# An H3 convolution with a feed-forward block on one core: short convolution on array halves, kept weight groups, and a new hand-off order

## The chip, the cores and the metric

The kernel runs on one core of one Trainium2 chip. The metric is the device time in microseconds of one execution. Before the change three runs gave 260.77, 261.48 and 261.54 us, median 261.48. Where a part of the program is meant, the engines are named as in the profile: PE is TensorE (PEld its weight loads), DVE is VectorE, ACT is ScalarE, POOL is GpSimd, SP is SyncE, which here only starts transfers.

## What is computed

All arrays are bfloat16: q, k, v of 2048 x 640, a short filter of 4 taps per channel, a long filter of 2048 taps per channel, and the feed-forward weights for F = 1728.

```
x = A_q;  q = layernorm(x)
k_shift = sum over t = 0..3 of k_pad[t : t + S] * shift_k[:, 3 - t]       # short causal convolution
kv = k_shift * v
y  = causal convolution of kv with ssm_k (length 2048)  +  kv * ssm_D
h  = x + q * y
h2 = h + (silu(layernorm(h) @ w_gate) * (layernorm(h) @ w_up)) @ w_down
```

## The kernel before

The sequence is cut into four blocks of 512. A block is held as 128 partitions of 4 rows (R = 4) of D = 640 = 5 x 128 columns. The feed-forward width is cut into seven groups of 256 columns (the last has 192), so 13 full chunks of 128 and a tail of 64.

The long convolution is done block by block by a discrete Fourier transform written as matmuls. For block j: the filter's block is loaded and transposed (g, gT), its spectrum G_j is made by matmuls with the constant WF (`spectrum`, line L375 in before, L353 after); the window H_j = G_j plus or minus G_(j-1) is formed on VectorE; kv_j comes from the short convolution and a multiply by v; its spectrum X_j is made in the same way; then the sums over i of X_i * H_(j-i) are accumulated in a spectrum A (`mac`: products L746, accumulations L747 in before; L619 and L622 after; L719 / L598 make the first products). The inverse transform (`inverse`: first sums on VectorE L823/L826, matmuls with WI L878; after L697/L700 and L748) gives y, which is multiplied into the normalised rows (L892 / L762) and added to x (h, L905 / L765). A layer norm follows, h is transposed (hT), and the feed-forward f_j runs: gate and up matmuls (L1022 / L852), ScalarE and VectorE turn them into the hidden tile tT (L1012, L1014, L1016), and the down projection (L1110 / L906) adds it up. f_j is written so that it lies beside the convolution work of block j+1.

A spectrum needs sums and differences of partial transforms. One of G_0's transforms is taken "directly" in before: a second constant matrix of 512 KB (`const_minus`, in tile tT) gives it by 16 more matmuls. The others get it from partial sums on VectorE.

The short convolution is done by TensorE with diagonal matrices of the taps. In block 0 each of the 4 row blocks takes 5 x 4 matmuls of 128 partitions and 128 columns (L639). In blocks 1 to 3 each row block takes 20 matmuls of 64 columns (L648): a tile T holds k twice, once shifted by a row, so that 128 partitions carry 64 channels at two taps. T's second half is made by a copy on ScalarE (L565) and transfers T<-T; the table `pairs` for it is filled on GpSimd (L1185) from taps turned by four small matmuls (L1175). Three "spins" of matmuls on constants (L1151, 18, 16 and 16) stand ahead of the real work.

What sets the order: every operation is recorded in a plan with a nominal duration in nanoseconds (for instance 1120 for one row block of L639, 640 for one of L648, named TWONS). The list ORDER gives the sequence in which they are handed to the engines; a negative number means that the operation takes its second engine. Each engine and each queue works in order, so ORDER fixes what stands behind what. Buffers are slots (12 'big' of 640 KB, 8 'S', 4 pairs of PSUM banks 'ps', 5 'row', 2 'co'), and a load must wait until its slot is free. In `add_into` a sum is made by a transfer that adds to its destination, issued by GpSimd (L278; after L255); a transfer of 640 KB is given 3830 ns in the new plan. Weight loads (L959 / L810) are issued by SP, or by GpSimd for blocks named in GLOAD.

Of the kernel before, what the change touches and what calls it, by code (L numbers as in the profile page):

```python
# [31 lines left out]
ADDLO = ('G1', 'G2', 'X1', 'X2', 'X3')  # L32
ADDMAC = ()
ADDWIN = (1,)
ADDH = (1, 2)
LEAD = {}
PAD = 16
DIRECT = ('G0',)
ACTLN = 0
ACTKV = 0  # L40
ACTLN2 = (0, 1, 2, 3)
LN1DVE = ()
LN2POOL = (1, 2)
HTURN = (1, 3, 2)
GTURN = (3,)
KTURN = (1, 2, 3)
SUM = {'X3': 'four', 'i2': 'four', 'i3': 'four', 'G3': 'four'}
ADDP = {(1, 1): ((0, 1),)}
ADDINV = (2,)
WHOLE3 = False  # L50
WARMUP = (18, 16, 16)
MERGE = ()
WIDE = ()
H1ACT = ()
PAIRED = True
K0TURN = False
EARLY = True
FFN4 = True
KVPAIR = ()
DPOOL = False  # L60
LASTCUT = 2
DIAGDVE = 4
ATURN = ()
GLOAD = (1, 2, 3, 'T')
FIRST = False
TWOTAPS = True
TWONS = 640
TCOPY = (1, 2)
# [43 lines left out]
HALVES = (ROWS[:2], ROWS[2:])  # L112


def make_basis():

# [96 lines left out]
def kernel(ctx: ExitStack, tc: tile.TileContext, A_q, A_k, A_v, A_shift_k, A_ssm_k, A_ssm_D, B_x,  # L213
# [369 lines left out]
    def load_k(j):  # L583
        if TWOTAPS and j:
            return load_two(j)
# [745 lines left out]
```

## Time and profile before

| what | value |
|---|---|
| median of 3 runs (lowest, highest) | 261.48 us (260.77, 261.54) |
| profiled execution: span from first to last instruction | 259.6 us |
| the rest of a run's median beside that span | 1.9 us |
| PE / DVE / ACT / POOL busy | 251.3 / 198.6 / 180.0 / 97.0 us |
| first feed-forward matmul | 49.70 us |
| last matmul ends, then last sum and store | 256.1 us, 3.5 us |
| bytes moved | 45.38 MB |
| granted TensorE clock | 1.000 |

The profile gives the span of the one execution that was profiled; its own time outside the span isn't listed, so times are compared through the 1.9 us. In the tables of groups a row has line, engine, operation, output and inputs, shape and count, then busy time and mean duration in ns, then the idle time just before and who ended it. In a timeline a row has start, length, engine, line, names, count. Matmuls overlap in the pipe, so the length of one is longer than the distance from its start to the next one's. The rows of waits give engine and line, whom it waited for, the total, how often, and the longest.

### The profile page before, as it was taken

The page shows a single profiled execution, that of the slowest core. Times are in us where ns is not written, and L with a number is a line of the kernel's source. Part 1 is how long each engine was busy: PE and PEld are TensorE (multiplying, and loading weights), DVE is VectorE, ACT ScalarE, POOL GpSimd, SP SyncE. Part 2 cuts the span into 40 slices and gives each one's busy share as a digit, 9 for nine tenths or more (in the row PEclk, how much of TensorE's full clock was granted, in tenths as well). Part 3 has the DMA queues.
Part 4 walks back from the last instruction along what each step waited for, and adds up shares of the span by engine and source line. Part 5 has one row for each costly group of instructions (what it writes and reads, how often), then busy time and mean ns, then how long its engine had stood idle before and what let it go on. Part 6 is the DMA issues. An engine that isn't in the chain of part 4 may idle for free.

```text
span 259.6 us, 4700 instructions
## 1 busy us (share of the span) xinstructions
PE 251.3 (97%) x1803; PEld 154.2 (59%) x1818; DVE 198.6 (77%) x259; ACT 180.0 (69%) x297; POOL 97.0 (37%) x115
## 2 busy tenths in 40 slices
PE   8999899999998999999999999999999999999994
PEld 7967577654654477754465477544456764444663
DVE  4679999999998999999999999999998200004403
ACT  2899999999998998569855985655497134637200
POOL 7961300008914199926117962240951022000000
PEclk9999999999999999999999999999999999999999
DMA  6997999979999998999997965994498546000002
GB/s 218 403 251 119 289 252 340 280 115 279 247 238 168 182 217 204 190 191 201 214 231 110 299 151 107 198 238 130 100 215 255 101 77 70 8 0 0 13 15 76
DMA packets 64752, 45.38 MB, mean 175 GB/s; under 512 B 31014, under 2 KB 60267, under 8 KB 64731
## 3 DMA queue, kind: packets, MB, share of 16 engines
q1 hardware_dynamic: 58896, 32.96, 51.1%
q0 software_dynamic: 5824, 12.13, 24.9%
q8 instruction: 14, 0.23, 0.4%
q14 instruction: 8, 0.06, 0.1%
q10 hardware_dynamic: 10, 0.01, 0.0%
HBM read 30.01 MB, written 4.59 MB: 133 GB/s over the span
## 4 chain that ended last, share of the span: by engine, by line
PE 78%; ACT 9%; DMA 6%; DVE 2%; issue 2%; SPq 1%; ACTq 0%; DVEq 0%
PE ps L1022 40%; PE ps L1110 23%; PE ps L375 10%; DMA big<-in_B_w_up_dram 4%; PE ps L878 3%; DMA big<-in_A_q_dram 3%; ACT T L565 2%; ACT big L364 1%; ACT S L364 1%; PE ps L648 1%; ACT row L757 1%; ACT big L664 1%; ACT big L473 1%; ACT tT L1014 1%; DVE row L892 1%
## 5 line engine op out<-in xcount | busy, mean ns | idle before, releaser
L1022 PE MATMUL ps<-big,big 128*128 128x512 bf16 x525 | 119.9, 379 | 1.7 <-DMA big<-in_B_w_up_dram 0.8
L1022 PEld LDWEIGHTS <-big 128*128 128x128 bf16 x540 | 52.5, 98 | 61.1 <-DMA big<-in_B_w_up_dram 1.3
L1110 PE MATMUL ps<-wd,tT 128*128 128x320 bf16 (+1 forms) x416 | 60.3, 299 | 0.0
L1110 PEld LDWEIGHTS <-tT 128*128 128x128 bf16 x416 | 40.7, 98 | 16.3
L1016 DVE TENSOR_TENSOR tT<-tT,co 128x2048 bf16<-128x2048 bf16 x12 | 14.5, 1219 | 34.4 <-ACT tT L1014 32.4
L375 PE MATMUL ps<-big,WF 128*128 128x320 bf16 x240 | 39.1, 299 | 1.3 <-ACT big L364 1.0
L1012 ACT CAST co<-ps 128x1024 bf16<-128x1024 f32 x24 | 24.2, 1011 | 17.3 <-PE ps L1022 16.8
L747 DVE TENSOR_TENSOR S<-S,big 128x2560 bf16<-128x2560 bf16 x23 | 34.3, 1492 | 1.2 <-DMA S<-big 0.5
L746 DVE TENSOR_TENSOR big<-S,S 128x2560 bf16<-128x2560 bf16 x23 | 34.1, 1485 | 0.2
L375 PEld LDWEIGHTS <-WF 128*128 128x128 bf16 x240 | 23.1, 97 | 12.8 <-issue 2.3
L1014 ACT ACTIVATE tT<-ps 128x1024 bf16<-128x1024 f32 x24 | 24.5, 1029 | 8.8 <-PE ps L1022 8.7
L757 ACT ACTIVATE row<-big 128x640 bf16<-128x640 bf16 x32 | 23.5, 742 | 1.8 <-DMA big<-in_A_q_dram 1.1
L807 ACT ACTIVATE row<-big,sm 128x640 bf16<-128x640 bf16 x23 | 20.3, 922 | 3.8 <-POOL sm L789 2.8
L1117 POOL DMA_DIRECT2D out_dram<-row x12 | 11.8, 1010 | 29.2 <-ACT row L1116 29.1
L364 ACT CAST S<-ps 128x320 bf16<-128x320 f32 (+1 forms) x36 | 19.4, 583 | 0.3
L1116 ACT CAST row<-ps 128x640 bf16<-128x640 f32 x12 | 8.1, 691 | 14.2 <-PE ps L1110 13.2
L364 ACT ACTIVATE big<-ps 128x640 bf16<-128x640 f32 (+1 forms) x24 | 15.6, 696 | 0.7 <-PE ps L375 0.7
L278 POOL DMA_DIRECT2D big<-row x8 | 7.0, 919 | 22.9 <-DVE row L892 22.9
L892 DVE SCALAR_TENSOR_TENSOR row<-row,ps 128x640 bf16<-128x640 bf16 x16 | 12.8, 815 | 1.1 <-PE ps L878 0.9
L278 POOL DMA_DIRECT2D S<-big x2 | 2.5, 1266 | 26.3 <-DVE S L719 19.1
L719 DVE TENSOR_TENSOR big<-S,S 128x2560 bf16<-128x2560 bf16 (+1 forms) x10 | 12.2, 1218 | 0.1
L959 POOL DMA_DIRECT2D big<-in_B_w_gate_dram x8 | 9.1, 1137 | 8.1 <-PE ps L1022 7.8
(110 smaller groups left out, 330.4 us busy)
## 6 DMA issues: line engine op xcount, KB each, us to landing
big<-in_B_w_up_dram SPq DMA_DIRECT2D x17, 320.0 KB, 5.1
big<-in_B_w_gate_dram SPq DMA_DIRECT2D x16, 320.0 KB, 4.7
big<-in_A_ssm_k_dram SPq DMA_DIRECT2D x4, 640.0 KB, 9.2
big<-in_A_q_dram SPq DMA_DIRECT2D x4, 640.0 KB, 7.6
big<-in_A_v_dram SPq DMA_DIRECT2D x4, 640.0 KB, 6.9
big<-in_B_w_gate_dram POOLq DMA_DIRECT2D x8, 320.0 KB, 7.2
big<-in_B_w_up_dram POOLq DMA_DIRECT2D x7, 320.0 KB, 6.7
wd<-in_B_w_down_dram SPq DMA_DIRECT2D x1, 2080.0 KB, 12.2
```

The source lines that it names most:

```text
L364: (lambda: nc.scalar.activation(dst(), src(), ACT.Copy, scale=2.0)) if twice else (lambda: nc.scalar.copy(dst(), src())),
L375: nc.tensor.matmul(ap(ps)[:, h, 0:NH], w, ap(src)[:, r, h * NH:(h + 1) * NH], start=(first and i == 0), stop=(last and i == len(rs) - 1), ...
L746: nc.vector.tensor_mul(flat2(b), X.part(xs), H.part(hs))
L747: f(A.part(dst), A.part(dst), flat2(b))
L757: act(825, lambda r=r, junk=junk: nc.scalar.activation(ap(junk), ap(x)[:, r, :], ACT.Square, scale=D ** -0.5, accum_out=sm(s, 1)[:, r:r + ...
L807: nc.scalar.activation(ap(row), ap(x)[:, r, :], ACT.Identity, bias=sm(s, 5)[:, r:r + 1], scale=sm(s, 4)[:, r:r + 1])
L892: nc.vector.scalar_tensor_tensor(two(ap(t)), two(ap(t)), 1.0, half(ap(ps)), op0=ALU.mult, op1=ALU.mult, accum_out=sm(s, 0)[:, r:r + 1])
L1012: act(1010, lambda ps=ps: nc.scalar.copy(ap(co)[:, at:at + 2, :], ap(ps)), src, [(co, gi % 2)])
L1014: act(1010, lambda ps=ps: nc.scalar.activation(ap(tT)[:, c:c + 2, :], ap(ps), ACT.Silu), src, [done(range(c, c + 2), ROWS)])
L1016: dve(1220, lambda: nc.vector.tensor_mul(ap(tT)[:, c - 2:c + 2, :], ap(tT)[:, c - 2:c + 2, :], ap(co)), [co], [done(range(c - 2, c + 2), R ...
L1022: nc.tensor.matmul(ap(ps)[:, i, :], ap(w)[:, k, off:off + P], ap(hT)[:, k, :], start=(k == 0), stop=(k == KT - 1))
L1110: nc.tensor.matmul(ap(ps)[:, hf, to:to + n], t, ap(wd)[:, c, col + (hf - hs[0]) * NH:col + (hf - hs[0]) * NH + n], start=(c == order[0]), ...
```

## The change

1. `DIRECT` is empty. G_0 gets its last part by two subtractions on VectorE as the other spectra do; the matrix `const_minus` and its load and the 16 matmuls with it go.
2. The short convolution has one form in all blocks. T holds k once. A row block takes 40 matmuls, each of 64 partitions by 64 columns, partitions 0 to 63 and 64 to 127 in turn, into two PSUM banks (L577). The plan gives it CONVNS = 680. Five diagonal pieces [128, 4, 64] replace both tables; ScalarE's doubling copy, the transfers T<-T, the `pairs` table and the four small matmuls go; a halo of 3 columns is copied instead. In block 0 the fill of the diagonals is 4 pieces on VectorE and 16 on GpSimd.
3. `KEEP = (3, 3, 3)`: the last three weight groups of a block stay in their slots, and odd blocks take the groups in reverse, so that these come first. 9 of 28 group loads go. GLOAD is (0, 1, 2, 3).
4. The third spin goes.
5. `sum_into` replaces `add_into`: any full sum may go to VectorE or to an adding transfer, and the product and the accumulation of `mac` are separate operations. Adding transfers of 640 KB: 4 before, 12 after (10 of them from a 'big' slot into a spectrum); of 160 KB (into h): 8 before, 4 after. VectorE's accumulations L747 / L622: 23 before, 14 after. Of the layer norms' small chains two more go from GpSimd to VectorE; 8 normalising steps move from ScalarE to VectorE; GpSimd issues 22 weight loads instead of 15.
6. ORDER is new: it was searched for the nominal durations alone.

```diff
-DIRECT = ('G0',)
+DIRECT = ()
-WARMUP = (18, 16, 16)
+WARMUP = (18, 16)
-GLOAD = (1, 2, 3, 'T')
-TWONS = 640
+GLOAD = (0, 1, 2, 3)
+KEEP = (3, 3, 3)
+CONVNS = 680
 ORDER = [
-    0, 2, 31, 1, 4, 5, 7, 10, 6, 8, 16, 13, 12, 11, 22, 29, 26, 37, 27, 14, 3, 15, 23, 28, 42, -39, 9, 35, -37, 24, 39, 205, 40,
...
+    0, 4, 2, 8, 1, 5, 21, 6, 52, 46, 50, 7, 48, 3, -48, 22, -52, 54, 14, 20, -54, -10, -14, 30, 18, 49, 28, 24, -30, -26,
...
-    def add_into(to, what, r, w, n=R * D):
-
-        plan.moved("add", P * n * 2, 1280, lambda: nc.gpsimd.dma_start(
-            out=to(), in_=what(), accum_op=ALU.add, max_dma_last_dim=2 * D * 2), r, w)
+    def sum_into(ns, fn, to, what, r, w, n=R * D, dma=False):
+
+        def by_dma():
+            nc.gpsimd.dma_start(out=to(), in_=what(), accum_op=ALU.add, max_dma_last_dim=2 * D * 2)
+        a, b = ("dve", ns, fn), ("add", 958.0 if n == D else 3830.0, by_dma)
+        if dma:
+            a, b = b, a
+        return plan.add(*a, r, w, (), b)
...
             def mm(r=r, out=out):
                 for c in range(KT):
                     for t in range(4):
+                        for b in range(2):
+                            at = slice(b * H2, (b + 1) * H2)
+                            if j:
+                                k = tk()[at, c, PAD + r - t:PAD + r - t + 4 * P - 3:4]
+                            else:
+                                q, off = (r - t, 1) if r >= t else (r - t + 4, 0)
+                                k = tk0()[at, c, q, off:off + P]
+                            nc.tensor.matmul(out()[:, b, c, :], k, ap(diag)[at, c, t, :], start=(t == 0), stop=(t == 3))
+            op = pe(CONVNS, mm, [of_t("H", *QUARTERS) if j else of_t(*FIRSTS), diag], [ps], [kv], 258)
...
-            def go(b=b, xs=xs, hs=hs, dst=dst, f=f):
-                nc.vector.tensor_mul(flat2(b), X.part(xs), H.part(hs))
+            dve(1490, lambda b=b, xs=xs, hs=hs: nc.vector.tensor_mul(flat2(b), X.part(xs), H.part(hs)), [X.at(xs), H.at(hs)], [b], [A.b])
+
+            def go(b=b, dst=dst, f=f):
                 f(A.part(dst), A.part(dst), flat2(b))
-            dve(3010, go, [X.at(xs), H.at(hs)], [b, A.at(dst)])
+            if f == nc.vector.tensor_add:
+                sum_into(1490, go, lambda dst=dst: A.part(dst), lambda b=b: flat2(b), [b], [A.at(dst)])
+            else:
+                dve(1490, go, [b], [A.at(dst)])
...
+        order = GROUPS if j % 2 == 0 else GROUPS[::-1]
+        for n, gi in enumerate(order):
...
+            if j == NB - 1 or n < NGRP - KEEP[j]:
+                kept.pop(gi)
```

Where the order moves, in three queues. First VectorE in the accumulation of block 2, before: each product (L746) is followed by its accumulation (L747) into the spectrum S_66.

```order
L746 TENSOR_TENSOR big_79<-S_68,S_70 128x2560
L747 TENSOR_TENSOR S_66<-S_66,big_79 128x2x1280
L746 TENSOR_TENSOR big_75<-S_71,S_65 128x2560
L747 TENSOR_TENSOR S_66<-S_66,big_75 128x2x1280
L746 TENSOR_TENSOR big_76<-S_71,S_65 128x2560
L747 TENSOR_TENSOR S_66<-S_66,big_76 128x2x1280
L746 TENSOR_TENSOR big_79<-S_71,S_65 128x2560
L747 TENSOR_TENSOR S_66<-S_66,big_79 128x2x1280
```

The same place after. S_66 is again the sum; big_76 and big_74 hold products that a transfer adds.

```order
L619 TENSOR_TENSOR big_76<-S_71,S_64 128x2560
L622 TENSOR_TENSOR S_66<-S_66,big_81 128x2x1280
L501 TENSOR_TENSOR S_68<-big_80,S_68 128x1280
L345 CAST big_83<-ps_92 128x640
L619 TENSOR_TENSOR big_81<-S_69,S_70 128x2560
L622 TENSOR_TENSOR S_66<-S_66,big_81 128x2x1280
L619 TENSOR_TENSOR big_74<-S_71,S_64 128x2560
L619 TENSOR_TENSOR big_82<-S_71,S_64 128x2560
L619 TENSOR_TENSOR big_81<-S_71,S_64 128x2560
L501 TENSOR_TENSOR S_68<-big_80,S_68 128x1280
L504 TENSOR_TENSOR S_68<-S_68,big_83 128x1280
L622 TENSOR_TENSOR S_66<-S_66,big_81 128x2x1280
```

Products without an accumulation behind them (big_76, big_74) are left to transfers; the last row waits until big_76 has been added.

GpSimd's queue in the same stretch, before, from the first transfers of block 2 to its one adding transfer (S_66 <- S_66).

```order
L563 DMA T<-T 64x5x512
L1117 DMA out_dram<-row_88 128x640
L959 DMA big_73<-in_B_w_gate_dram 128x5x256
L563 DMA T<-T 64x5x514
L1117 DMA out_dram<-row_87 128x640
L278 DMA S_66<-S_66 128x2x1280
L959 DMA big_82<-in_B_w_gate_dram 128x5x256
L959 DMA big_80<-in_B_w_up_dram 128x5x256
```

After: four adding transfers into S_66 (L255), with a memset ahead of them and two weight loads (L810) between.

```order
L255 DMA big_82<-row_85 128x640
L970 MEMSET tail 64x512
L255 DMA S_66<-big_72 128x2x1280
L255 DMA S_66<-big_73 128x2x1280
L810 DMA big_73<-in_B_w_up_dram 128x5x256
L810 DMA big_73<-in_B_w_gate_dram 128x5x256
L255 DMA S_66<-big_76 128x2x1280
L255 DMA S_66<-big_74 128x2x1280
```

The weight loads go into slot big_73, so they wait until the transfer that adds big_73 has landed, and the next two adds stand behind them.

SP's first entries, before:

```order
L597 DMA T<-in_A_k_dram 128x2560
L330 DMA big_73<-in_A_ssm_k_dram 128x5x512
L342 DMA big_74<-in_A_q_dram 128x2560
L337 DMA big_75<-in_A_v_dram 128x2560
L1199 DMA WF<-const_wf 128x2048
L342 DMA big_76<-in_A_q_dram 128x2560
L1205 DMA tT_84<-const_minus 128x2048
```

and after:

```order
L308 DMA big_72<-in_A_ssm_k_dram 128x5x512
L514 DMA big_74<-in_A_k_dram 128x2560
L977 DMA WF<-const_wf 128x2048
L320 DMA big_75<-in_A_q_dram 128x2560
L315 DMA big_76<-in_A_v_dram 128x2560
L810 DMA big_78<-in_B_w_up_dram 128x5x64
L308 DMA big_80<-in_A_ssm_k_dram 128x5x512
```

The long filter comes first, then k and WF, and TensorE turns g ahead of k and runs 18 of G_0's matmuls before the short convolution of block 0. The first feed-forward matmul now stands behind all of X_1, G_1, G_2 and the short convolution of block 2: 160 L353 matmuls stand ahead of it (156 L375 before) and 480 matmuls of L577 (80 of L639 and 80 of L648 before).

More of the change, by code (lines that the diff above doesn't have):

```diff
@@ L578, in plain, with load_k, both @@
[L578 to L598 removed]
+    def load_k(j):
+        if j == 0:
+            k = new("ld")
+            load(MB, 5120, lambda: nc.sync.dma_start(out=rd(k), in_=block(kk, j)), [k])
+            return k
+        tiny = plan.add("pool", 600, lambda: nc.gpsimd.tensor_copy(*both()), [halo if j == 1 else of_t(("A", R - 1))], [of_t("H")], (),
+                        ("act", 240, lambda: nc.scalar.copy(*both())))
+        def both():
+            return tk()[:, :, PAD - 3:PAD], ap(halo) if j == 1 else tk()[:, :, TW - 3:TW]
+        turns = []
+        for a in range(R):
+            turns.append(transfer(MB / 4, lambda a=a: nc.sync.dma_start(
+                out=tk()[:, :, PAD + a * P:PAD + (a + 1) * P], in_=kk[j * BLK + a * P:j * BLK + (a + 1) * P, :], transpose=True),
+                [], [of_t(("A", a))]))
+        if j == 1:
+            for op in [tiny] + turns:
+                op.deps.update(firsts)
+        return T
@@ L600, in turned_k @@
     def turned_k(k, behind=None, table=None):
-        if plan.block in KTURN or not plan.block and K0TURN:
+        if plan.block:
             return k
-        src = rd if plan.block else plain
-        kT = T if TWOTAPS else new("kT")
         for r in range(R):
@@ L630, in kv_of, with by_half, out, mm @@
+        return T
+    firsts = []
+    def kv_of(j, v, behind=None):
+        if j == 0:
+            dve(60, lambda: nc.vector.memset(tk0()[:, :, :, 0:1], 0.0), [], [of_t("K0")])
         kv = new("t4")
-        for r in (0, 2, 1, 3) if plan.block in KVPAIR else range(R):
+        def by_half(t):
+            return t.rearrange("p (c b x) -> p b c x", c=KT, b=2)
+        for r in range(R):
             ps = conv_ps()
-            def mm(r=r, ps=ps):
+            def out(ps=ps):
+                return half(ap(ps)).rearrange("p b (c x) -> p b c x", c=KT)
+            def mm(r=r, out=out):
@@ L707, in mac, with straight @@
-    def mac(A, X, H, first, pieces=((0, 1),), adds=(), at=None):
-        if at in MERGE:
-            merged(A, X, H, first, [a for a in adds if isinstance(a, int)])
-            return
-        adds = [a for a in adds if not isinstance(a, int)]
+            if j == 0:
+                firsts.append(op)
+            def straight(r=r, out=out):
+                nc.vector.tensor_mul(by_half(ap(kv)[:, r, :]), out(), by_half(rd(v)[:, r, :]))
+            op = plan.add("act", 700, lambda r=r, out=out: nc.scalar.copy(by_half(ap(kv)[:, r, :]), out()), [ps, v], [(kv, r)], (), ("dve", 820, straight))
@@ L807, in scalar @@
             nc.scalar.activation(ap(row), ap(x)[:, r, :], ACT.Identity, bias=sm(s, 5)[:, r:r + 1], scale=sm(s, 4)[:, r:r + 1])
-        if bias and plan.block >= ACTLN or not bias and plan.block in ACTLN2:
-            plan.add("act", 930, scalar, [(x, r), s], [row], holds, ("dve", 450, vector))
-        else:
-            dve(450, vector, [(x, r), s], [row], holds)
+        plan.add("act", 930, scalar, [(x, r), s], [row], holds, ("dve", 450, vector))
     def inverse(A, x, n1, pieces=((0, 1),), minus=None, groups=(ROWS,)):
@@ L932, in load_w @@
     def load_w(gi):
[L933 to L944 removed]
+        if gi in kept:
+            return kept[gi]
         w = new("wgu")
@@ L1080, in ffn @@
-        first, then = ROWS[:2], ROWS[2:]
-        for gi in range(0, lead, 2):
-            chunks((gi, gi + 1), first)
-        for gi in range(lead, NGRP - 1):
-            by_four(gi) if FFN4 else chunks((gi,), ROWS)
-        behind = odd_by_four() if FFN4 else odd_chunks()
-        for gi in range(0, lead, 2):
-            behind = chunks((gi, gi + 1), then)
+        order = GROUPS if j % 2 == 0 else GROUPS[::-1]
+        for n, gi in enumerate(order):
+            if gi == NGRP - 1:
+                last = odd_by_four()
+            else:
+                close = gi // 2 in [g // 2 for g in order[:n]]
+                if not close:
+                    co = new("co")
+                last = by_four(gi, co, close)
+            if j == NB - 1 or n < NGRP - KEEP[j]:
+                kept.pop(gi)
@@ L1088, in ffn @@
+        behind = last
         for r in ROWS:
             ps = new("ps_f")
-            order = list(range(lead * 2, NCH)) + list(range(lead * 2))
+            order = list(range(NCH))
             last = end and r == ROWS[-1]
@@ L1190 @@
     plan.add("pool", 600, lambda: nc.gpsimd.memset(ap(wd)[64:P, NC_FULL, :], 0.0), [ident], [(wd, "zero")])
-    turns = [op for op in plan.ops if op.eng in ("turn", "aturn")]
     first("Lx0")
     x = load_x(0)
-    if FIRST:
-        plan.ops[-1].then.update(turns)
     first("Lv0")
@@ L1212 @@
     first("k0")
-    k = turned_k(k, spun, table)
-    again = spun
-    if not K0TURN:
-        again = spin(WARMUP[2])
-        again.deps.update(op for op in plan.ops if op.name == "k0" and op.eng == "pe" and op is not again)
-    kv = kv_of(0, k, None, v, again)
+    turned_k(k, spun, table)
+    kv = kv_of(0, v)
     first("g0")
@@ L1248 @@
         stage("Lk")
[L1249 removed]
+        load_k(j)
         stage("Lv")
@@ L1287 @@
         stage("i")
-        s = inverse(A, x, n1, groups=HALVES if LEAD.get(j) else (ROWS,))
+        s = inverse(A, x, n1)
         stage("t")
```

404 lines of the change are left out of this document (77 added, 327 removed), and 72 rows, old and new, of the table ORDER.

## The prediction

> **What bounds the kernel now.** I read the head of the page, then TensorE's share by stage, then its waits. The columns of the windows are the length and, for each engine, the busy time.
>
> ```profile
> span 259.6 us, 4700 instructions
> PE 251.3 (97%) x1803; PEld 154.2 (59%) x1818; DVE 198.6 (77%) x259; ACT 180.0 (69%) x297; POOL 97.0 (37%) x115
> ```
>
> ```profile
> 0.00:49.70 49.70, 46.63 (x507) 36.39 (x508) 41.84 (x94) 42.92 (x93) 19.42 (x44) 1.00 1.00 265
> 49.70:256.10 206.40, 204.67 (x1298) 117.80 (x1311) 156.38 (x166) 137.05 (x205) 77.54 (x71) 1.00 0.72 155
> 256.10:259.60 3.50, 0.00 (x0) 0.00 (x0) 0.41 (x1) 0.00 (x0) 0.00 (x0) 1.00 0.20 67
> ...
> 49.70:100.00 50.30, 49.20 (x340) 28.18 (x343) 48.89 (x46) 48.18 (x77) 24.59 (x20) 1.00 1.02 221
> 100.00:150.00 50.00, 49.74 (x346) 29.04 (x350) 49.25 (x50) 36.91 (x51) 29.10 (x29) 1.00 0.96 199
> ```
>
> ```profile
> PE ps L375 <- ACT big L364: 1.0, 2, 0.8
> ...
> PE ps L1022 <- DMA big<-in_B_w_up_dram: 0.8, 1, 0.8
> ...
> DVE S L747 <- DMA S<-big: 0.5, 1, 0.5
> ```
>
> TensorE is the bound: 204.67 us of the 206.40 behind the first feed-forward matmul (49.70), then 3.5 us for the last sum and store. VectorE is almost as full: 48.89 of 50.30 and 49.25 of 50.00 us. So matmul time that goes comes off the end, as long as VectorE, which has no room, does not become late. One wait on a transfer that adds (0.5 us) is already there.
>
> **The change part by part.** First the matmuls.
>
> ```profile
> L648 PE MATMUL ps<-pairs,T 128*128 128x64 bf16 x240 | 9.2, 197 | 0.2 <-DVE big L658 0.2
> L639 PE MATMUL ps<-big,T 128*128 128x128 bf16 x80 | 4.6, 219 | 0.0
> L375 PE MATMUL ps<-big,tT 128*128 128x320 bf16 x16 | 3.3, 298 | 0.0
> L1175 PE MATMUL ps<-ident,row 5*128 5x5 bf16 x4 | 0.2, 164 | 0.0
> ```
>
> ```profile
> 6.56 1.10 PE L1151 MATMUL ps<-const-bfloat16-1.0 128*128 128x128 bf16 x16
> 7.50 1.00 PE L471 MATMUL ps<-ident,big 128*128 128x128 bf16 x15
> 8.34 4.63 PE L639 MATMUL ps<-big,T 128*128 128x128 bf16 x80
> 12.80 1.04 PE L375 MATMUL ps<-big,WF 128*128 128x320 bf16 x6
> ...
> 37.06 1.49 PE L648 MATMUL ps<-pairs,T 128*128 128x64 bf16 x40
> 38.39 0.71 PE L375 MATMUL ps<-big,WF 128*128 128x320 bf16 x4
> ...
> 112.03 1.79 PE L375 MATMUL ps<-big,WF 128*128 128x320 bf16 x12
> 113.66 16.35 PE L1022 MATMUL ps<-big,big 128*128 128x512 bf16 x73
> 129.85 0.33 PE L648 MATMUL ps<-pairs,T 128*128 128x64 bf16 x5
> ```
>
> A mean of 197 ns is the depth of the pipe; what counts is the distance from start to start. The DFT matmul takes (113.66 - 112.03)/12 = 0.136 us, the two-tap matmul (38.39 - 37.06)/40 = 33 ns, so 0.665 us for a row block of 20, and block 0's convolution (12.80 - 8.34) = 4.46 us.
> - First G from partial sums: 16 of the L375 matmuls go, -2.17 us.
> - The third spin: 7.50 - 6.56, -0.94. The four L1175 matmuls: -0.2.
> - The convolution: a row block becomes 40 matmuls of 64 partitions, two halves in turn. No row shows that form. Lower bound: the two halves fully beside each other and bound by their 64 columns, 0.136 x 64/320 x 20 = 0.54 us. Upper bound: each of the 40 at the 33 ns of the two-tap form, 1.33 us. I take 0.68, the number in the kernel's own table (CONVNS), as the same table gives 0.64 where the rows show 0.665 and 1.12 where they show 4.46/4 = 1.115. Beside the two ends the Trainium skill, "TensorE: Matmul & The Clock Gate", has two rules: section "Wait — 56ns, not 53.3ns?" puts the least distance of matmul starts near 25 ns however small they are, by which a piece would take 40 x 25 = 1.0 us (an estimate) and the sum would be +0.2 instead of -4.87; "The mechanism" of Part 3 lets matmuls on different row groups start some 4 ns apart, by which it stays near the lower end. The 33 ns row agrees with the first and can't tell on the second. Block 0: 4 x 0.68 - 4.46 = -1.74; the other twelve row blocks: 12 x (0.68 - 0.665) = +0.18.
>
> Sum -4.87 us. By the order, 20 DFT matmuls (2.7 us) and block 2's convolution also move ahead of the first feed-forward matmul, so ahead of it TensorE's work changes by +0.4 us and behind it by -5.3. The start-up costs nothing net: GpSimd's 16 diagonal pieces come before the first convolution now.
>
> ```profile
> 6.97 5.00 POOL L1185 TENSOR_SCALAR pairs<-row,taps 128x64 bf16<-128x64 bf16 x12
> ...
> L719 DVE TENSOR_TENSOR S<-S,S 128x1280 bf16<-128x1280 bf16 x4 | 3.3, 821 | 0.0
> ...
> L789 DVE TENSOR_TENSOR sm<-sm 128x4 f32<-128x4 f32 x2 | 0.3, 164 | 0.1
> ```
>
> At 0.42 us each, sixteen take 6.7 us; begun near 3.5 they end at 10.2, where the convolution began at 8.34 before. It is 1.74 shorter, and the 18 forward matmuls that stand ahead of it fill 2.4 us. Without that cover it is +1.9. The two new subtractions of G0 (0.82 us each) fall where VectorE has 49.70 - 41.84 = 7.9 us free; uncovered they are 1.6.
>
> The nine of 28 weight groups not loaded again take transfers away but only one wait of 0.8 us was a weight; I count none of it and leave 0.8 as a gain for the low end. Three doubled copies of T leave ScalarE, which waits for TensorE anyway; nothing.
>
> Now what VectorE hands to transfers. Eight more sums of 640 KB go through GpSimd's queue, twelve in place of four.
>
> ```profile
> S<-big POOLq DMA_DIRECT2D x2, 640.0 KB, 8.3
> ...
> DMA to landing us min/median/max: 2.9/5.9/9.9
> ...
> L959 POOL DMA_DIRECT2D big<-in_B_w_gate_dram x8 | 9.1, 1137 | 8.1 <-PE ps L1022 7.8
> ```
>
> ```profile
> 59.46 1.28 POOL L278 DMA_DIRECT2D S<-big  x1 [19.05 <-DVE S L719]
> ...
> 66.06 1.49 DVE L747 TENSOR_TENSOR S<-S,big 128x2560 bf16<-128x2560 bf16 x1
> 67.47 1.48 DVE L746 TENSOR_TENSOR big<-S,S 128x2560 bf16<-128x2560 bf16 x1
> 69.43 1.49 DVE L747 TENSOR_TENSOR S<-S,big 128x2560 bf16<-128x2560 bf16 x1 [0.47 <-DMA S<-big]
> 70.96 1.49 DVE L823 TENSOR_TENSOR big<-S 128x2560 bf16<-128x2560 bf16 x1
> 72.37 0.48 DVE L665 TENSOR_TENSOR big<-big,big 128x640 bf16<-128x640 bf16 x1
> 72.77 1.48 DVE L518 TENSOR_TENSOR S<-S,S 128x2560 bf16<-128x2560 bf16 x1
> ...
> 78.26 1.22 DVE L1016 TENSOR_TENSOR tT<-tT,co 128x2048 bf16<-128x2048 bf16 x1
> 79.40 0.81 DVE L892 SCALAR_TENSOR_TENSOR row<-row,ps 128x640 bf16<-128x640 bf16 x1
> ```
>
> One add took 9.9 us from issue (59.46) to landing; with the median of the two at 8.3 the other took 6.7. These are the ends. VectorE's steps: 1.41 us for 2560 columns (66.06 to 67.47), 0.40 for 640, 1.14 for 2048.
> - Block 1: the new order puts 7.6 us of VectorE work (four products and sums, two small multiplies, one gate) between the product that is added by transfer and the accumulation that waits for it. Late by 0 to 2.3 us. From the last copy of transposed h to the inverse's first sum VectorE has 18 x 1.41 + 2 x 1.14 + 4 x 0.40 + 0.4 = 29.7 us. TensorE has two convolution pieces (1.4) and 135 feed-forward matmuls at 0.216 (16.19 us over 75, two of which the trace misses) = 30.6. So TensorE waits 0 to 1.4.
> - Block 2 is worse, because GpSimd's queue is in order. Count from the end of the second product that is to be added. That add is issued at 0 and lands at 6.7 to 9.9. The next two entries are weight loads into the buffer that it frees; each holds the queue 1.1 us, so the third add goes out at 9.0 to 12.2 and lands at 15.7 to 22.1. VectorE reaches the accumulation that needs it after 18.0 us (nine steps of 1.41, three of up to 0.82, ten tiny ones of 0.16, two more of 0.8 and 0.4). Late by 0 to 4.1; a like count of steps leaves 0.7 of slack at that inverse (an estimate): 0 to 3.4 on the path.
>
> At the median landing both together cost 0.2 us, at the slow end 4.8. The slow add fell in the stretch with a transfer share of 1.02, where the new ones fall too, so I go beyond the median: +1.5. Queued behind the late accumulation are VectorE's eviction multiplies and TensorE's inverse; that is how it reaches the end.
>
> Sum: 259.6 - 4.87 + 1.5 = 256.2 us for the span; the median of the runs shown stands 261.48 - 259.6 = 1.9 above the span, so **258.1 us**.
>
> **The rivals.**
> 1. All adds hidden: 259.6 - 4.87 + 1.9 = 256.6; with the weight wait gone 255.8. For it: the median landing. Against it: the 0.5 us that one add in two already cost.
> 2. The halves do not run beside each other: 16 x (1.33 - 0.68) = +10.4, less the waits that this slower TensorE hides (1.5): 267.0; half way, at 1.0 us and with the same 1.5 hidden, 261.7. It decides from 0.68 + (261.5 - 258.1)/16 = 0.89 us for a row block. Against it speaks only the table's fit. The floor of the Trainium skill's page quoted above is the half-way case.
> 3. The array empties whenever its partition is changed: twelve convolution pieces, 24 changes, each at most what a lone small matmul takes beyond its spacing (197 - 33 ns = 0.164): +3.9, so 262.0. No row shows such a change, since before has none. The Trainium skill, "TensorEngine Tiling (Array Packing)", Key Properties, speaks for both sides: tiles load weights and multiply in parallel, which is against rival 2, but changing the tiling mode drains the array, which is this one.
> 4. Slower by the queue: GpSimd's add behind the weight loads lands at its late end, 22.1 us, in block 2, and the same in block 3: 4.8 us as above gives 254.7 + 4.8 + 1.9 = 261.4, and 2 us more where block 3's slack is spent too 263.4. It decides from 4.9 us of carried waits.
>
> **How the numbers follow.** Forecast 0.40 (own range 257.0 to 260.6), rival 1 0.15, rival 2 0.15, rival 3 0.10, rival 4 0.20. About 0.3% (0.8 us) is what a measurement can tell from no change. Faster: rival 1 and nearly all of the forecast, 0.53. Same (260.7 to 262.3): the lower parts of rivals 2 to 4, 0.11. Slower 0.36. The range leaves out rival 2's full price and the gain below 255.5: 255.5 to 264.
>
> **What would show it.** Convolution pieces of 40 matmuls 0.65 to 0.72 us from start to start, and full-array matmuls right behind them without a gap; last matmul at about 252.6; TensorE waiting for the first sum of blocks 1 and 2's inverse by some tenths to 2 us, VectorE's accumulations waiting for S<-big transfers by 1 to 5 us in all. I am wrong if the pieces take over 0.89, or if VectorE's waits for adds sum to over 6 us.

## The result, and the profile after

The changed kernel took 269.38 us in the median of four runs (267.06 to 269.86), the kernel before 261.12 us: a ratio of 1.030, with a 95% interval of 1.0253 to 1.0347. It is slower by some 8 us where 258.1 us were forecast, and lies outside the range. Its profiled execution has a span of 268.2 us, 8.6 more than before. Ratios and their intervals, here and below, leave out executions over 1.5% above the fastest of the same kernel (one of them took 1465 us), while medians are of all.

The head of the page of the changed kernel, and TensorE by stage. The windows start with the first feed-forward matmul, at 53.35 us.

```profile
span 268.2 us, 5201 instructions
PE 251.6 (94%) x2088; PEld 150.1 (56%) x2102; DVE 198.4 (74%) x279; ACT 164.8 (61%) x281; POOL 78.9 (29%) x98
...
0.00:53.35 53.35, 47.78 (x810) 36.43 (x810) 42.93 (x89) 43.25 (x92) 17.84 (x37) 1.00 0.89 256
53.35:100.00 46.65, 45.93 (x259) 25.05 (x258) 45.44 (x45) 36.66 (x59) 13.49 (x16) 1.00 0.78 168
100.00:130.00 30.00, 25.35 (x163) 14.17 (x164) 29.06 (x34) 15.72 (x29) 14.48 (x15) 0.89 1.03 201
```

TensorE is busy as long as before (251.6 against 251.3 us), in a longer span. The third window is the place that is new: 25.35 of 30.00 us, and a granted clock of 0.89, where all stages of before had 1.00. The waits of TensorE there and at the start, and VectorE's waits for adding transfers:

```profile
PE ps L852 <- DMA big<-row: 4.4, 1, 4.4
PE ps L577 <- issue: 2.5, 2, 1.6
...
PE ps L906 <- DVE row L923: 0.6, 1, 0.6
...
PE ps L748 <- DVE big L697: 0.5, 1, 0.5
PE ps L852 <- ACT tT L843: 0.5, 1, 0.5
...
DVE S L622 <- DMA S<-big: 2.1, 3, 1.1
```

In order of time, TensorE at the convolution of blocks 0 and 1, at the first feed-forward matmul, and between the feed-forwards of blocks 0 and 1:

```profile
13.37 1.40 PE L577 MATMUL ps<-diag,T 64*128 64x64 bf16 x83
15.66 0.71 PE L577 MATMUL ps<-diag,T 64*128 64x64 bf16 x37 [0.90 <-issue]
16.30 3.52 PE L353 MATMUL ps<-big,WF 128*128 128x320 bf16 x22
...
27.61 0.86 PE L577 MATMUL ps<-diag,T 64*128 64x64 bf16 x40
28.40 0.72 PE L353 MATMUL ps<-big,WF 128*128 128x320 bf16 x4
...
31.31 0.72 PE L577 MATMUL ps<-diag,T 64*128 64x64 bf16 x32
33.62 1.00 PE L577 MATMUL ps<-diag,T 64*128 64x64 bf16 x48 [1.59 <-issue]
...
53.35 6.87 PE L852 MATMUL ps<-big,big 128*128 128x512 bf16 x30
...
111.48 0.43 PE L906 MATMUL ps<-wd,tail 128*128 128x320 bf16 x2
116.35 0.59 PE L852 MATMUL ps<-big,big 128*128 128x512 bf16 x1 [4.43 <-DMA big<-row]
117.15 12.48 PE L852 MATMUL ps<-big,big 128*128 128x512 bf16 x48 [0.22 <-issue]
129.57 0.62 PE L577 MATMUL ps<-diag,T 64*128 64x64 bf16 x26
```

A lone convolution piece of 40 matmuls takes 28.40 - 27.61 = 0.79 us. Twice TensorE stops in the middle of a piece for "issue", that is, for nothing that this view shows. At 111.95 block 0's feed-forward is done and block 1's has to wait 4.43 us for its transposed h. The clock falls while it waits:

```profile
111.95:114.30 2.35, 0.00 (x0) 0.00 (x0) 2.35 (x2) 1.05 (x4) 0.67 (x1) 1.00 1.09 268
114.30:121.10 6.80, 4.53 (x11) 1.71 (x13) 6.63 (x7) 3.67 (x8) 3.90 (x4) 0.50 1.06 206
121.10:130.00 8.90, 8.90 (x66) 4.11 (x66) 8.54 (x8) 3.28 (x4) 6.28 (x8) 1.00 0.97 235
```

2.35 us after TensorE went idle the clock is 0.50, for 6.8 us; of the 4.75 us after 116.35 half is lost, 2.4 us. The Trainium skill, "TensorE: Matmul & The Clock Gate", section "What's actually happening", says that the clock is halved after about one idle window of 3.4 us, which runs freely. The trace agrees in part: 6.8 us are two such windows, but the fall came after 2.35 us, before a whole window had been idle.

Where the 8.6 us came from, in the forecast's terms. Ahead of the feed-forward +3.65 us (53.35 against 49.70): two stops 2.5, convolution pieces 0.9 longer than 12 x 0.68, and the 0.4 that was forecast; these make 3.8. Behind it +5.0 instead of -5.3, so 10.3 of difference: the wait for h with the short gap behind it 4.65, the low clock 2.4, block 3's convolution 0.9 (3.6 instead of 2.7), and single waits of at most 0.6 us for most of the rest.

### The profile page after: what moved, and what is told of

Its sections match the earlier page's. It is cut to its first block, busy times and chain, and to the rows that moved or that the text cites. A ratio compares the mean times of both kernels' runs of the same rounds, so it can differ in the third digit from the quotient of the medians.

```text
span 268.2 us, 5201 instructions
## 1 busy us (share of the span) xinstructions
PE 251.6 (94%) x2088; PEld 150.1 (56%) x2102; DVE 198.4 (74%) x279; ACT 164.8 (61%) x281; POOL 78.9 (29%) x98
## 4 chain that ended last, share of the span: by engine, by line
PE 62%; DVE 15%; DMA 9%; issue 8%; ACT 4%; POOL 1%; DVEq 0%; POOLq 0%; ACTq 0%
PE ps L852 29%; PE ps L906 16%; PE ps L353 8%; DMA big<-row 4%; PE ps L577 4%; DMA S<-big 3%; PE ps L748 2%; DMA row<-in_A_ssm_D_dram 2%; DVE S L598 2%; DVE row L762 2%; DVE tT L846 2%; DVE S L700 1%; DVE big L619 1%; DVE S L622 1%; DVE big L697 1%
## 5 line engine op out<-in xcount | busy, mean ns | idle before, releaser
L353 PE MATMUL ps<-big,WF 128*128 128x320 bf16 x240 | 38.6, 299 | 0.3 <-ACT big L342 0.2
L843 ACT ACTIVATE tT<-ps 128x1024 bf16<-128x1024 f32 x24 | 24.3, 1022 | 20.9 <-PE ps L852 20.7
L619 DVE TENSOR_TENSOR big<-S,S 128x2560 bf16<-128x2560 bf16 x24 | 35.1, 1484 | 0.0
L353 PEld LDWEIGHTS <-WF 128*128 128x128 bf16 x240 | 22.7, 98 | 10.0 <-issue 1.2
L255 POOL DMA_DIRECT2D S<-big x10 | 12.3, 1233 | 49.7 <-DVE big L619 34.3
L622 DVE TENSOR_TENSOR S<-S,big 128x2560 bf16<-128x2560 bf16 x14 | 20.8, 1489 | 2.4 <-DMA S<-big 2.1
L810 POOL DMA_DIRECT2D big<-in_B_w_up_dram x11 | 10.8, 983 | 33.6 <-PE ps L748 12.7
L342 ACT ACTIVATE big<-ps 128x640 bf16<-128x640 f32 (+1 forms) x30 | 17.5, 621 | 2.3 <-PE ps L353 2.3
L913 POOL DMA_DIRECT2D out_dram<-row x12 | 12.9, 1256 | 20.3 <-ACT row L912 20.3
L342 ACT CAST S<-ps 128x640 bf16<-128x640 f32 (+1 forms) x28 | 16.1, 617 | 1.1 <-PE ps L353 0.8
L684 ACT ACTIVATE row<-big,sm 128x640 bf16<-128x640 bf16 x15 | 13.5, 920 | 3.9 <-DVE sm L666 3.5
L577 PE MATMUL ps<-diag,T 64*128 64x64 bf16 x640 | 13.0, 194 | 2.6 <-issue 2.5
L577 PEld LDWEIGHTS <-T 64*128 64x128 bf16 x640 | 11.6, 110 | 6.2 <-issue 5.7
```

The costliest lines, as they stand in the source:

```text
L342: (lambda: nc.scalar.activation(dst(), src(), ACT.Copy, scale=2.0)) if twice else (lambda: nc.scalar.copy(dst(), src())),
L353: nc.tensor.matmul(ap(ps)[:, h, 0:NH], w, ap(src)[:, r, h * NH:(h + 1) * NH], start=(first and i == 0), stop=(last and i == len(rs) - 1), ...
L577: nc.tensor.matmul(out()[:, b, c, :], k, ap(diag)[at, c, t, :], start=(t == 0), stop=(t == 3))
L619: dve(1490, lambda b=b, xs=xs, hs=hs: nc.vector.tensor_mul(flat2(b), X.part(xs), H.part(hs)), [X.at(xs), H.at(hs)], [b], [A.b])
L622: f(A.part(dst), A.part(dst), flat2(b))
L843: act(1010, lambda ps=ps: nc.scalar.activation(ap(tT)[:, c:c + 2, :], ap(ps), ACT.Silu), src, [done(range(c, c + 2), ROWS)])
```

## The experiments

**The convolution as 20 full-array matmuls.** Each row block takes two taps into each bank:

```diff
-                        for b in range(2):
-                            at = slice(b * H2, (b + 1) * H2)
+                        b = t // 2
...
-                            nc.tensor.matmul(out()[:, b, c, :], k, ap(diag)[at, c, t, :], start=(t == 0), stop=(t == 3))
+                        nc.tensor.matmul(out()[:, b, c, :], k, ap(diag)[:, c, t, :], start=(t % 2 == 0), stop=(t % 2 == 1))
```

> The changed kernel with its short convolution written as 20 full-array matmuls of 128 partitions by 64 columns per row block (two taps into each bank), in place of 40 on halves: the sums over taps and halves are not the right ones, everything else stays. Theory A, the convolution on halves costs by itself (two stops of TensorE for instructions, 2.5 us, and changes of the array's shape, some 1.8 us over 0.68 a piece): the stops are gone, a piece takes 0.665 us, the first feed-forward matmul moves from 53.35 to about 50 us and the run is 3.5 to 4.5 us faster than the changed kernel (269.4), about 265. Rival B, the start is set by VectorE's and ScalarE's chain: the first feed-forward matmul stays within 1 us of 53.35 and the run stays at 268.5 or above.

Measured: 262.71 us, ratio to before 1.0057 (1.0024 to 1.009). In its timeline a lone piece, and the start of the feed-forward:

```profile
26.19 0.83 PE L576 MATMUL ps<-diag,T 128*128 128x64 bf16 x20
26.85 0.71 PE L353 MATMUL ps<-big,WF 128*128 128x320 bf16 x4
...
49.68 6.64 PE L851 MATMUL ps<-big,big 128*128 128x512 bf16 x29
...
110.45 0.38 PE L851 MATMUL ps<-big,big 128*128 128x512 bf16 x1 [2.28 <-DMA big<-row]
```

Theory A: a piece takes 0.66 us, no stop is left, the feed-forward starts at 49.68 as before. The convolution on halves alone cost the 3.7 us at the start. The gain, 6.7 us, is larger than expected, as the wait for h is 2.3 us here instead of 4.4, and the clock behind it is at 0.50 for 3.4 us instead of 6.8.

**The halves one after the other.** The same 640 matmuls, 20 of one half and then 20 of the other:

```diff
-                for c in range(KT):
-                    for t in range(4):
-                        for b in range(2):
+                for b in range(2):
+                    for c in range(KT):
+                        for t in range(4):
```

> The changed kernel with the same 640 convolution matmuls, but all 20 of the lower half of a row block first and then the 20 of the upper half, not in turn. If the halves run beside each other only because they alternate, a piece takes 40 x 33 ns = 1.33 us instead of 0.72 to 0.79 and the matmuls in the first 53 us take 7 us longer. If TensorE works through the list at the same rate either way, pieces stay at 0.7 to 0.8 us.

Measured in one run: 273.21 us. A lone piece in its timeline:

```profile
28.47 1.42 PE L577 MATMUL ps<-diag,T 64*128 64x64 bf16 x40
29.82 0.72 PE L353 MATMUL ps<-big,WF 128*128 128x320 bf16 x4
```

1.35 us, 34 ns a matmul, close to the upper bound of the prediction; and no stop within a piece. So of these two orders the halves run beside each other only in the one that alternates between them, and it is the fast list that stops.

**One part alone in the kernel before.** Block 0's convolution on halves, all else as before, and the same without the third spin:

```diff
-                        nc.tensor.matmul(line(ap(ps))[:, c * P:(c + 1) * P], k,
-                                         ap(diag)[:, 4 * c + t, :], start=(t == 0), stop=(t == 3))
+                        for b in range(2):
+                            at = slice(b * H2, (b + 1) * H2)
+                            nc.tensor.matmul(half(ap(ps))[:, b, c * H2:(c + 1) * H2], k[at],
+                                             ap(diag)[at, 4 * c + t, at], start=(t == 0), stop=(t == 3))
```

> The kernel before with one part of the change alone: block 0's short convolution as 160 matmuls on halves instead of 80 on the full array, all else as before. By the price seen in the changed kernel (0.72 for the piece, 0.9 us for a stop) 4.46 becomes 2.7 to 3.8 us; as 18 spins and 35 transposes go ahead of it, the stop for instructions may move. If TensorE's start carries to the end: 0.5 to 1.7 us faster than before. Rival: VectorE's multiplies and the start chain set the first feed-forward matmul, it stays at 49.7 and the time is the same within 0.4 us.

> The kernel before with block 0's convolution on halves and without the third spin, which takes 32 instructions out of TensorE's list ahead of it. With the spin the convolution stopped 2.7 us after 130 of 160 matmuls, at about the 448th instruction of the list, the place where the changed kernel also stopped. Theory A, the stop is at a place in the list (instructions not yet fetched): it comes 16 matmuls later, after about 146. Rival B, it waits for data or an engine: it stays after about 130 or goes.

Measured: with the spin 263.22 us, ratio 1.0057 (1.0021 to 1.0092); without it 263.78 us in one run. The two timelines, first with, then without the spin:

```profile
9.17 2.07 PE L641 MATMUL ps<-big,T 64*128 64x64 bf16 x130
13.93 0.98 PE L641 MATMUL ps<-big,T 64*128 64x64 bf16 x30 [2.69 <-issue]
14.84 1.78 PE L375 MATMUL ps<-big,WF 128*128 128x320 bf16 x6
```

```profile
8.20 2.30 PE L641 MATMUL ps<-big,T 64*128 64x64 bf16 x146
13.66 0.38 PE L641 MATMUL ps<-big,T 64*128 64x64 bf16 x14 [3.16 <-issue]
```

Sixteen matmuls less ahead of it, and the stop comes exactly sixteen matmuls later: 130, then 146. Counted from the start of TensorE's list (93 matmuls stand ahead of the convolution with the spin, 77 without it), both stops are behind the 223rd matmul; as a matmul and its weight load are two instructions, that is about instruction 448. The changed kernel's first stop, after 96 + 40 + 4 + 83 matmuls, is behind the 223rd too, its second behind the 478th (about instruction 958). So the stop belongs to a place in the list, not to data. In both kernels the profile has an instruction queue that moves blocks of 16 KB, before and after (packets, MB, share):

```profile
q8 instruction: 14, 0.23, 0.4%
```

```profile
q8 instruction: 16, 0.26, 0.4%
```

They serve 3621 and 4190 matmuls and weight loads of TensorE: one block for some 260. The Trainium skill, "Runtime: NRT & Kernel Launch", section "Instruction fetch mechanics", says that a list is fetched in blocks of 16 KiB or 256 instructions and that crossing a block is mostly hidden. The block size agrees with these counts; hidden it was not, where two instructions went every 17 ns: stops of 0.9, 1.6, 2.7 and 3.2 us.

The records of that queue in the traces tie the stops to the blocks. In the changed kernel a block landed at 14.44 and one at 32.20 us, and TensorE went on at 15.66 and 33.62. With halves in block 0 alone the block landed at 12.62 and TensorE went on at 13.93; without the spin at 12.32 and 13.66. The lag is 1.2 to 1.4 us each time. Where the list came to the same place later than that, nothing stopped: with the halves one after the other the block landed at 14.26, and TensorE passed the place at 16.3. So TensorE waited for instructions, and a stop is as long as TensorE is early.

Halves in block 0 cost more than they save: the piece of 160 matmuls runs from 9.17 to 14.84, 5.7 us, against 4.46 before. The theory's own price, 2.7 to 3.8, was too low, as the stop was 2.7 instead of 0.9 and the clock was at 0.50 for 3.4 us behind it; the first feed-forward matmul came at 52.01 us instead of 49.70.

**The third spin alone.** `WARMUP = (18, 16, 0)` in the kernel before.

> The kernel before without its third spin of 16 matmuls. If TensorE's list sets the start, 0.94 us are won, as the prediction counted; if the g that the transposes behind the spin wait for lands only then, nothing is won, and if the clock is not yet at 1.0 without it, it is slower.

Measured: 260.28 us against 261.42, ratio 0.9967 (0.9945 to 0.9989). Two rows of its timeline, and one of the kernel before:

```profile
7.61 1.00 PE L471 MATMUL ps<-ident,big 128*128 128x128 bf16 x15 [0.64 <-DVE T L614]
...
49.81 1.24 PE L1022 MATMUL ps<-big,big 128*128 128x512 bf16 x4
```

```profile
81.11 1.25 PE L1022 MATMUL ps<-big,big 128*128 128x512 bf16 x4 [0.78 <-DMA big<-in_B_w_up_dram]
```

The kernel before without that spin is faster than both kernels, but this does not bear out the term of the sum, -0.94 us. Without the spin TensorE waits for VectorE's copy into T instead, and the first feed-forward matmul is at 49.81 us against 49.70: the spin had filled a wait, and at the start nothing is won. What is missing in this profile is the wait of 0.78 us for a weight at 81 us. Of the 19 executions of the kernel before beside it seven took 260.13 to 260.68 us and twelve 261.17 to 262.32; all ten without the spin took 259.95 to 260.51. That the weight's wait is what parts them is not shown.

**The clock.** Eighteen matmuls on constants ahead of block 1's feed-forward:

```diff
+            if fill and op.eng == "pe" and op.name == "f1pe":
+                fill = False
+                ps = [b for b in op.bufs if b.tag == "ps"][0]
+                for _ in range(18):
+                    nc.tensor.matmul(ap(ps)[:, 0, :], nc.const_aps.tensor(1.0, [P, P], BF16),
+                                     ap(WF).rearrange("p r c q -> p (r c q)")[:, 0:BLK], start=True, stop=True)
```

> The changed kernel with 18 matmuls on constants put ahead of block 1's first feed-forward matmul, where TensorE waits 4.4 us for the transposed h and the granted clock then is 0.5 for 6.8 us. Theory A, the clock fell because TensorE stood idle: it stays at 1.0 there, the matmuls behind run at 0.216 us again and 2 to 2.5 us are won (about 267.2). Rival B, the clock falls for another reason or at another place: it is below 1.0 for some 6.8 us again and the time stays within 0.5 us of 269.4, or the 18 matmuls cost 3.9 us.

Measured: 267.56 us, ratio to before 1.0266 (1.0197 to 1.0335). The clock was 1.000 over the whole profiled span, and 0.998 to 1.000 in all four executions, against 0.985 to 0.994 in the changed kernel:

```profile
114.48 4.05 PE L1070 MATMUL ps<-WF,const-bfloat16-1.0 128*128 128x512 bf16 x17
119.25 5.12 PE L852 MATMUL ps<-big,big 128*128 128x512 bf16 x23 [0.72 <-DMA big<-row]
```

The fall came from the idle time. The median is 1.8 us lower, with an interval that overlaps that of the changed kernel, so the size is less sure than the cause. In that profile VectorE also waited 5.9 us for adding transfers and TensorE 2.9 for a first sum, where the changed kernel's own profile has 2.1 and 0.5: the landing of these adds varies. The clock did not fall behind these 2.9 us.

**The adding transfers.** Accumulations that go by transfer are given back to VectorE at the same place, first block 2's four, then all ten:

```diff
-            if n < 0:
+            if n < 0 and not (op.other[0] == "add" and op.name in ("m12", "m22")):
                 op.eng, op.ns, op.fn = op.other
```

> The changed kernel with block 2's four large accumulations that go by adding transfers done by VectorE at the same place in the order. Theory A, these transfers and the weight loads queued behind them hold up the four transposes of block 1's h (landing 4 to 6.2 us instead of 2.6): the wait of 4.4 us ahead of block 1's feed-forward falls to 1 to 2.5 us and the clock's dip shrinks or goes; VectorE has 5.6 us more to do in block 2, of which the inverse of block 2 feels up to 4. Net between -4 and +1 against 269.4. Rival B, the transposes are late because the norm ahead of them is late on VectorE (102.9 us): the wait stays above 3.5 us and the time rises by the 2 to 4 us that VectorE gets.

> The changed kernel with all ten accumulations that go from a product by an adding transfer done by VectorE at the same place in the order. If the late adds (VectorE's waits, the rival of GpSimd's queue in the prediction) are a large part of the 8 us: VectorE's 2.1 us of waits go but 14 us of sums come, in stretches that are full: between -1 and +6 against 269.4. If the adds slow the transposes of h by their load, the wait of 4.4 us falls below 2. If neither: the wait stays at 4 to 5 us and the time rises by what VectorE has no room for.

Measured: 269.87 us (ratio 1.0334, 1.0273 to 1.0394) with block 2's four, 277.19 us (1.0614, 1.0543 to 1.0685) with all ten, the last case of its expectation. In both the wait for h is still there; in the first:

```profile
116.79 0.59 PE L852 MATMUL ps<-big,big 128*128 128x512 bf16 x1 [4.88 <-DMA big<-row]
```

and 4.17 us in the second. The last transpose of h still landed 6.7 and 6.5 us after its issue, against 6.2 in the changed kernel. The adding transfers are neither what held up h nor what made the kernel slow; with all ten sums on VectorE it is slower by 8 us. Rival B of the first run was right about the wait and wrong about the price, since VectorE took block 2's four sums at no measurable cost.

**The norm forward.** Block 1's norm of h, its squares and normalising steps moved up in the order, its sums into h by VectorE; once with the transposes moved too, once with them behind block 3's filter transposes; each also with the 20 full-array matmuls:

```diff
 ORDER = [
...
-    -292,
+    291, 292, 295, 294,
...
+    -297,
+    303, 301, -300, 297,
```

(the moved entries only; the numbers are those of the operations).

> The changed kernel with block 1's norm of h taken forward: three of its sums into h by VectorE instead of adding transfers, the three squares on ScalarE right behind them, the norm on VectorE ahead of three products and a sum of block 2, and the normalising steps and transposes right behind it. Nothing else moves. Theory A, the wait of 4.4 us and the fall of the clock behind it come from the place of this norm in the order: the transposes are issued some 5 us earlier, the wait goes, the clock stays at 1.0, and 5 to 7 us are won against 269.4 (about 263). Rival B, the transposes are slow because of the transfers around them: a wait of 2 us or more stays and less than 3 us are won.

> The edits of the run with 20 full-array matmuls per row block and of the run with block 1's norm forward, together; the convolution's sums are again not the right ones. Theory A, the two causes are apart and add up: 262.7 less the wait of 2.3 and the 1.8 us of low clock, so 258 to 259, near the 256.6 that the sum of matmuls gives without any wait. Rival B, another wait takes their place: 260.5 or above.

> As the run that took block 1's norm forward, but the transposes of h stay behind block 3's filter transposes in SP's queue, which that run had pushed behind them (TensorE then stood 20.8 us for them). Theory A, the place of the norm is what makes h late: transposes start near 99 us instead of 104.8, the wait of 4.4 us and the clock's fall go, and 5 to 7 us are won against 269.4. Rival B, transposes that run beside other transfers take 4 to 10 us whenever they are issued: 2 us or more of wait stay, less than 3 us are won.

> The 20 full-array matmuls per row block (sums not the right ones) and the norm of block 1 forward as in the run beside it. Theory A, the two causes add up: 258 to 259.5, below the kernel before (261.4). Rival B, another wait takes their place: 260.5 or above.

Measured: 288.61 and 285.79 us, then 280.01 and 275.71 us (ratios 1.1058, 1.0937, 1.0714 and 1.0574). In the first pair TensorE stood 20.8 us (20.7 with the full-array matmuls) for the transposed filter of block 3, which SP's queue now had behind the transposes of h. In all four VectorE stood 14.4 to 15.6 us for a slot that a store of the output had not yet left, because that store was queued behind them (issued at 93.1 us in the changed kernel, at 108.0 in the last of the four). The first row is of the first run, the second of the last:

```profile
PE ps L315 <- DMA big<-big: 20.8, 1, 20.8
```

```profile
DVE big L580 <- DMA out_dram<-big: 15.6, 1, 15.6
```

The two theories could not be told apart; what these runs show is that a few entries moved by hand change the slots and the queues more than they win.

**The wait for h taken away.** Block 1's first six chunks read a constant in place of h:

```diff
+                early = j != 1 or len(begun) >= 6
+                begun.extend([1] if j == 1 else [])
                 for k in range(KT):
-                    nc.tensor.matmul(ap(ps)[:, i, :], ap(w)[:, k, off:off + P], ap(hT)[:, k, :], start=(k == 0), stop=(k == KT - 1))
+                    x = ap(hT)[:, k, :] if early else ap(WF)[:, k % R].rearrange("p c q -> p (c q)")
+                    nc.tensor.matmul(ap(ps)[:, i, :], ap(w)[:, k, off:off + P], x, start=(k == 0), stop=(k == KT - 1))
```

> The changed kernel in which block 1's first six feed-forward chunks (30 matmuls, 6.5 us) read the constant WF in place of the transposed h, so that TensorE needn't wait for it there; their products are left out of the result in effect. Theory A: block 1's feed-forward begins when block 0's ends, the wait of 4.4 us and the 2.4 us of low clock go, and the time falls by 6 to 7 us to 262.5 to 263.5. Rival B, VectorE's chain sets the pace behind it too and another wait takes the place: above 266.

> The same with the convolution as 20 full-array matmuls per row block (sums not the right ones). Theory A, start and transposed h are the whole of the difference: 262.7 less the wait of 2.3 and 1.8 us of low clock, 258 to 259.5. Rival B: another wait takes their place, 260.5 or above.

Measured: 264.16 us (ratio 1.0134, 1.0097 to 1.017), and with the full-array convolution 260.44 us (0.9964, 0.9937 to 0.9991). The waits of TensorE in the second:

```profile
PE ps L855 <- ACT row L915: 3.0, 2, 1.6
...
PE ps L909 <- DVE row L926: 0.6, 1, 0.6
PE ps L855 <- ACT tT L843: 0.5, 1, 0.5
```

Alone the two causes are worth 6.7 and 5.2 us, together 9 (269.4 to 260.4): they overlap, and together they cover the whole loss. Without them the change is level with the kernel before, 0.4% below it by the ratio. But it is not the 256.6 us that the sum gives without waits, nor the 258 to 259.5 of theory A: 3.0 us of a wait for ScalarE's eviction of the output take their place. Rival B (260.5 or above) is the nearer. The run with the halves, 264.16 us, lies between its two theories, with a wait of 1.8 us for the same eviction.

## Why the prediction was wrong, point by point

- **"So matmul time that goes comes off the end, as long as VectorE, which has no room, does not become late."** This step failed, in the condition that it named. The prediction counted VectorE's slack at the inverses of blocks 1 and 2, and those waits were as small as it said (0.5 us and less). It did not count the longer chain from block 0's to block 1's transposed h: sums, inverse, norm and transposes. Before, TensorE took 113.66 - 49.70 = 64.0 us from the start of feed-forward 0 to that of feed-forward 1 and didn't wait for h. After, its list for the same stretch is 111.95 - 53.35 = 58.6 us, 5.4 shorter as forecast, but h came at 63.0. From the start of feed-forward 0 to the issue of the last transpose of h, VectorE (the third busy time) is full in both kernels, and as long:

```profile
49.70:106.76 57.06, 55.96 (x390) 33.03 (x393) 55.48 (x51) 52.71 (x83) 30.95 (x27) 1.00 1.01 208
```

```profile
53.35:110.06 56.71, 55.99 (x333) 32.30 (x332) 55.12 (x62) 42.91 (x69) 15.24 (x18) 1.00 0.83 167
```

That last transpose landed after 4.9 us at most before, and after 6.2 us in the changed kernel. The 5.3 us that were to be won behind the feed-forward's start ran into a chain as long as before. That this chain, and not the adding transfers, set it is shown by the runs that took these away and left the wait; which of its members would have to go was not settled, since moving the norm brought other waits.
- **The convolution's term.** A lone piece between full-array matmuls took 0.79 us, two in a row 1.45 (51.90 to 53.35): 0.66 for a piece, as the 0.68 has it, and 0.13 for each of the twelve stretches. That fits rival 3, the change of the array's shape, at some 1.6 us and not 3.9. Rival 2, halves that do not overlap, was wrong for this list and right for one that doesn't alternate. The rule of 25 ns from the Trainium skill, "TensorE: Matmul & The Clock Gate", section "Wait — 56ns, not 53.3ns?", did not bind here: 40 matmuls in 0.66 to 0.79 us start 17 to 20 ns apart, on the two halves in turn.
- **What no term had: stops for instructions.** 2.5 us in the changed kernel. The profile of before could not show them, as its list never went through instructions that fast.
- **What no term had: the clock.** Behind the wait of 4.43 us the clock was at 0.50 for 6.8 us, behind the 2.28 us of the full-array run for 3.4 us; behind 1.6 us in the changed kernel and 1.8 us in the run without the wait for h it did not fall. The prediction priced waits at their length.
- **The adding transfers, +1.5.** VectorE waited 2.1 us for them, within the 1 to 5 forecast, and little reached TensorE. Rival 4, GpSimd's queue, did not decide anything: with block 2's adds off it the time stayed the same.
- **The spin (-0.94), G0 (16 matmuls) and the diagonals' cover** came out right in their sum: with the convolution at 0.66 the feed-forward starts at 49.68, where 49.70 + 0.4 was the forecast. That is in part luck, as the spin alone won nothing at the start; the other terms were not measured one by one.
- **The signal.** It was written that pieces over 0.89 us or waits for adds over 6 us would prove it wrong. On the whole neither happened: the sixteen pieces took 0.79 on average, though two of block 3 took 1.0, and the adds were waited for 2.1 us. The test was set on two terms, and a third place decided.

## What to carry to other kernels

Where a second engine is almost full, work taken off the bound engine moves the end only as far as the second engine's whole chain allows; count that chain from one hand-over to the next, not only at the nearest one. Many small matmuls are paid in instructions too: look where a fast stretch of the list lies, and whether the engine stops there for "issue". Count a wait on TensorE of a few microseconds with the low clock that can follow it. And before the price of a filler is counted as won, look for the wait that it may be filling.

## What was not expected of the hardware

- TensorE stops at fixed places of its instruction list (448, 958) when small matmuls run through it at some 17 ns each, until 1.2 to 1.4 us after a block of instructions has landed: 0.9 to 3.2 us a stop; at 34 ns there was none within a piece.
- Two halves of the array ran beside each other when the list took them in turn, and not one after the other: 0.79 us against 1.35 us for the same 40 matmuls.
- A stretch of half-array matmuls between full-array ones cost about 0.13 us beyond its pieces (0.79 against 0.66 for one piece).
- The clock fell to 0.50 after 2.35 us without work and stayed there for 6.8 us, 4.75 of them after work had come back.
